# Value casts moved off GpSimd, weight loads released by small gates, and a searched order for the front of an attention and mixture-of-experts kernel

## The chip, the cores and the metric

The kernel runs on one core of one Trainium2 chip. The metric is the device time of one launch in microseconds (us). Engine names are those of the profile: PE is TensorE (PEld its weight loads), DVE is VectorE, ACT is ScalarE, POOL is GpSimd and SP is SyncE, which here only issues transfers. Times are medians over several runs. A ratio is the mean time of one kernel's fast runs over the mean of the other's in the same rounds, so it is not quite the ratio of the medians that stand beside it. A time is about 1.8 us more than the span that the profile shows for the same execution.

## The reference

Shortened here (the logits keep their maximum subtracted, the constants of the scaling are left out):

```python
def _attn_ref(q, k, v):                       # 8 samples, 8 heads, 576 positions, 64 wide
    phi = lambda x: np.where(x > 0, x, np.exp(x) - 1.0) + 1.0
    q_p, k_p = phi(q), phi(k)
    kv = np.einsum('bhsd,bhse->bhde', k_p, v)
    z = np.sum(k_p, axis=2)
    num = np.einsum('bhsd,bhde->bhse', q_p, kv)
    den = np.einsum('bhsd,bhd->bhs', q_p, z)[..., None] + 1e-06
    return num / den
def _moe_ref(x, w_gate, w1, w2):              # x 4608 x 512, 8 experts, 1024 hidden
    P = np.exp(x @ w_gate - max)              # then 8 rounds of row and column scaling
    ...
    for e in range(8):
        out += P[:, e:e+1] * (np.maximum(x @ w1[e], 0) @ w2[e])
```

## The kernel before

A planner in the kernel's own Python takes a list of tasks, each with an engine, a modelled duration, its dependencies and a rank (`prio`). It simulates the engines and emits every task on its engine in the order of that simulation. Only the order comes from it. On the chip each engine runs its list in that order, and waits come from the tiles.

```python
pick = ...   # of the tasks that can start first on this engine: the lowest (prio, id)
t["fn"](e)   # emit it
```

The front is attention in 16 half batches (sample b, four heads g). TensorE does it interleaved with the two layers of expert 0. The loads of half batches 2 and 3 are issued by GpSimd, the others by SyncE, and the value cast is on GpSimd:

```python
(nc.gpsimd if n in (2, 3) else nc.sync).dma_start(out=<kin, qin, vin>, in_=...)
...
tvv.append(fadd(("pool", 1.3), f_v, deps=[ta, tin["v"]], use=[gvv, gin["v"]], prio=pr))   # fp32 -> fp16
...
w_t = {0: load_w1(0, prio=-290.0, parts=2, deps=[vcast[0]])}       # w1 of expert 0
w_t[0] += load_w2(0, prio=-96.5, parts=2, deps=[in_prev[0]])       # w2, behind half batch 3's loads
w_t[1] = load_w1(1, prio=0.0, after=110.0) + load_w2(1, prio=0.0, after=115.0)
```

The softmax here doesn't subtract the row's maximum and nothing guards it: scores larger than these inputs give would overflow.

## Time and profile before

| | before |
|---|---|
| time, median of 3 | 981.74 us (981.48 to 982.49) |
| the profiled execution | 983.97 us, span 982.2 |
| TensorE busy | 98% of the span |
| VectorE, ScalarE, GpSimd busy | 79%, 57%, 13% |

This document uses, as the prediction does, the **unused TensorE time** of a stretch, because a busy share hides small holes. It is the stretch's length less the sum over its matmuls of their start-to-start time when nothing is waited for (0.2167 us for 128x512, 0.109 for 128x256, and so on). It counts waits, half-speed stretches and warm-up alike. A matmul that crosses a cut is counted in both stretches. So a value can be slightly negative, and sums over many stretches come out too low (27.5 us up to 120 us in the first profile of before, 29.8 if each matmul is counted once). Differences between two kernels move by up to 0.7 us for this reason.

### The profile page before, as it was taken

To read this page: it belongs to the slowest core of one execution; us is meant where nothing else is said; L and a number is where in the kernel's file an instruction comes from. 1 tells how busy PE (TensorE), PEld (TensorE's weight loads), DVE (VectorE), ACT (ScalarE), POOL (GpSimd) and SP (SyncE) were. 2 spreads that over 40 slices of the span, in tenths; PEclk is the share of its full clock that TensorE was granted. 3 is DMA by queue.
4 is the path that set the end of the run, shared out by engine and by line. 5 is a ranking of instruction groups with operands and counts; after the bars stand their busy time and mean duration, and the time that the engine had idled before them with its cause. 6 is when DMAs were issued, how large, how long until landed. Compare 5 with 4: busy or idle time off the path is not lost.

```text
span 982.2 us, 21403 instructions
## 1 busy us (share of the span) xinstructions
PE 962.2 (98%) x8716; PEld 792.7 (81%) x8716; DVE 771.7 (79%) x1561; ACT 563.2 (57%) x1034; POOL 127.9 (13%) x171
## 2 busy tenths in 40 slices
PE   7899999999999999999999999999999999999997
PEld 4455564488888888888888888888888888888885
DVE  6898869967777777777777777777777777777774
ACT  4798754565555555555555555555555555555552
POOL 4111200001111111111111111111111111111110
PEclk9999999999999999999999999999999999999999
DMA  9886953162226312272225322272225322236663
GB/s 318 257 303 239 265 160 140 65 127 77 75 76 142 97 73 76 76 161 76 77 75 137 101 76 75 76 162 76 76 76 137 102 76 76 76 103 168 161 161 98
DMA packets 47029, 121.99 MB, mean 124 GB/s; under 512 B 4177, under 2 KB 18001, under 8 KB 46929
## 3 DMA queue, kind: packets, MB, share of 16 engines
q1 hardware_dynamic: 32128, 99.76, 30.3%
q0 software_dynamic: 14480, 20.33, 11.5%
q8 instruction: 68, 1.11, 0.5%
q10 hardware_dynamic: 320, 0.52, 0.1%
q14 instruction: 33, 0.26, 0.1%
HBM read 119.69 MB, written 17.69 MB: 140 GB/s over the span
## 4 chain that ended last, share of the span: by engine, by line
PE 89%; DVE 1%; ACT 1%; issue 0%
PE ye L809 33%; PE hq L627 23%; PE att L627 11%; PE Zye L627 6%; PE Zye L809 6%; PE ye L706 5%; PE hq L536 4%; PE xt_ps L387 0%; PE kv_ps L306 0%; PE num_ps L371 0%; PE lg_ps L405 0%; DVE tk L281 0%; PE qt_ps L332 0%; ACT tq L272 0%; PE den_ps L347 0%; ACT qpT L221 0%
## 5 line engine op out<-in xcount | busy, mean ns | idle before, releaser
L823 DVE SCALAR_TENSOR_TENSOR acc<-ye,P_sb,acc 128x256 f32<-128x256 f32 x620 | 264.9, 477 | 95.3 <-PE ye L809 77.9
L627 PEld LDWEIGHTS <-W 128*128 128x128 f16 x2016 | 197.1, 98 | 23.7
L809 PEld LDWEIGHTS <-S 128*128 128x128 f16 x1984 | 194.1, 98 | 22.7 <-issue 0.3
L809 PE MATMUL ye<-T,S 128*128 128x256 f16 x1488 | 192.8, 273 | 0.1
L833 POOL TENSOR_TENSOR acc<-acc,st 128x256 f32<-128x256 f32 x124 | 87.5, 725 | 625.6 <-ACT st L830 620.7
L653 ACT ACTIVATE h<-hq 128x512 f16<-128x512 f32 x126 | 76.3, 606 | 160.8 <-PE hq L627 160.8
L627 PEld LDWEIGHTS <-w 128*128 128x128 f16 x1512 | 147.6, 98 | 23.3 <-issue 1.0
L809 PEld LDWEIGHTS <-h 128*128 128x128 f16 x1488 | 145.6, 98 | 16.8
L627 PE MATMUL hq<-xs,W 128*128 128x256 f16 x1008 | 151.2, 273 | 0.0
L627 PE MATMUL att<-xs,W 128*128 128x256 f16 x1008 | 151.2, 272 | 0.0
L627 PE MATMUL hq<-xs,w 128*128 128x256 f16 x1008 | 140.7, 272 | 0.8 <-DVE h L656 0.8
L782 DVE TENSOR_TENSOR S<-h 128x1024 f16<-128x1024 f16 x124 | 85.4, 688 | 57.9 <-ACT h L653 57.9
L656 DVE CUSTOM_DVE_ANT_0 h<-att,s 128x512 f16<-128x512 f32 x126 | 86.7, 688 | 13.1 <-ACT s L643 13.1
L830 ACT ACTIVATE st<-Zye,P_sb 128x256 f32<-128x256 f32 x124 | 52.1, 471 | 78.0 <-PE Zye L809 78.0
L643 ACT COPY s<-hq 128x512 f32<-128x512 f32 x126 | 75.0, 595 | 36.7 <-PE hq L627 36.7
L650 ACT ACTIVATE h<-Zye 128x512 f16<-128x512 f32 x126 | 75.2, 597 | 35.1 <-PE Zye L627 35.1
L656 DVE CUSTOM_DVE_ANT_0 h<-hq,s 128x512 f16<-128x512 f32 x126 | 86.5, 686 | 0.8 <-PE hq L627 0.7
L639 ACT COPY Zye<-hq 128x512 f32<-128x512 f32 x126 | 73.3, 581 | 16.3 <-PE hq L627 16.3
L706 PE MATMUL ye<-w,h 128*128 128x512 f16 x320 | 77.6, 379 | 0.9 <-DVE acc L223 0.9
L627 PE MATMUL Zye<-xs,w 128*128 128x256 f16 x504 | 75.6, 273 | 0.0
L647 ACT COPY s<-att 128x512 f32<-128x512 f32 x126 | 74.5, 591 | 0.0
L536 PE MATMUL hq<-xT,w 128*128 128x512 f16 x288 | 70.6, 379 | 2.4 <-ACT h L540 2.2
(90 smaller groups left out, 963.1 us busy)
## 6 DMA issues: line engine op xcount, KB each, us to landing
xs<-xd SPq DMA_DIRECT2D x63, 896.0 KB, 4.6
w<-in_moe_w_dram POOLq DMA_DIRECT2D x14, 1024.0 KB, 11.7
out_dram<-acc SPq DMA_DIRECT2D x68, 128.0 KB, 2.4
kin<-in_k_dram SPq DMA_DIRECT2D x14, 576.0 KB, 6.0
qin<-in_q_dram SPq DMA_DIRECT2D x14, 576.0 KB, 5.0
vin<-in_v_dram SPq DMA_DIRECT2D x14, 576.0 KB, 6.4
xd<-xst SPq DMA_DIRECT2D x9, 512.0 KB, 2.6
xd<-xT SPq DMA_DIRECT2D x9, 256.0 KB, 7.1
```

Source lines behind the costliest of these rows:

```text
L536: nc.tensor.matmul(ghq["tile"], lhsT=gw1["tile"][:, c, ts(f, P)], rhs=xT[:, c, ds(512 * g, 512)], start=(c == 0), stop=(c == NDT - 1))
L627: nc.tensor.matmul(dst[:, p, :], lhsT=lhs(p, c), rhs=rhs(c), start=(first and p == 0 and c == 0), stop=(c == 1), skip_group_check=True)
L643: nc.scalar.copy(out=gs2["tile"], in_=gX["tile"])
L647: nc.scalar.copy(out=gs5["tile"], in_=gR["tile"])
L650: nc.scalar.activation(out=hd(0, 0), in_=Zt[1], func=AF.Relu)
L653: nc.scalar.activation(out=hd(1, 0), in_=gX["tile"], func=AF.Relu)
L656: nc.vector._custom_dve(TENSOR_ADD_SAT, out=dst, in0=ps, in1=sb, s0=3.0e38, s1=0.0)
L706: nc.tensor.matmul(gy[tt]["tile"], lhsT=gh["tile"][:, f, ds(P * tt, P)], rhs=gw2["tile"][:, f, :], start=(f == 0), stop=(f == NFT - 1))
L782: nc.vector.tensor_tensor(out=Sx[:, i], in0=a0, in1=a1, op=op)
L809: nc.tensor.matmul(bank(g_)[:, s, :], lhsT=lhs(s, kk), rhs=rhs(kk), start=(new and s == 0 and kk == 0), stop=(kk == 3), skip_group_check=True)
L823: nc.vector.scalar_tensor_tensor(out=dst(), in0=bank(g_)[:, s, :], scalar=P_sb[:, gg, e:e + 1], in1=dst(), op0=ALU.mult, op1=ALU.add)
L833: nc.gpsimd.tensor_tensor(out=dst(), in0=dst(), in1=gst["tile"], op=ALU.add)
```

## The change

Its intent is to take the casts off GpSimd, where they hold VectorE up, to let GpSimd issue weights when a four-column copy has seen some value tile arrive, to split the first two layer-1 blocks in halves, to give the exp tiles a third buffer, and to replace the ranks of some 260 tasks by values found in an off-line search over the planner's own model.

```diff
-    p_e = S_.pool(2)
+    p_e = S_.pool(3)                                   # exp tiles, also bufs=3
-        tvv.append(fadd(("pool", 1.3), f_v, ...))
+        tvv.append(fadd(("act", 1.17) if n < 2 else ("dve", 0.75), f_v, ...))
+        if n in (0, 13, 15):
+            def f_gate(_):
+                nc.gpsimd.tensor_copy(out=gate, in_=gin["v"]["tile"][:, 0, 0, 0:4])
+            gates[n] = add(("pool", 0.15), f_gate, deps=[tin["v"]], use=[gin["v"]], prio=pr)
-    w_t = {0: load_w1(0, prio=-290.0, parts=2, deps=[vcast[0]])}
+    w_t = {0: load_w1(0, prio=-290.0, parts=2, deps=[gates[0]])}
+        if g == 0:                                     # layer 1: two halves for the first two blocks
+            jobs = [(f, c, c + 2) for c in (0, 2) for f in range(2)] + jobs[2:]
-    w_t[1] = load_w1(1, prio=0.0, after=110.0) + load_w2(1, prio=0.0, after=115.0)
+    w_t[1] = load_w1(1, prio=0.0, deps=[gates[13]]) + load_w2(1, prio=0.0, deps=[gates[15]])
+    ranks = """
+        45:-90.9997 68:-96.9976 69:-91 70:-97.006 ...      (task:rank[:engine]; cut)
+        ... 1060:8.3482 1061:-97.003 1063:-89.9994
+    """
+    for w in ranks.split():  ...  t["prio"] = float(p)
```

## The prediction

> **What bounds the kernel now.** I read the page first: busy shares, the slices, the chain that ended last.
>
> ```profile
> PE 962.2 (98%) x8716; PEld 792.7 (81%) x8716; DVE 771.7 (79%) x1561; ACT 563.2 (57%) x1034; POOL 127.9 (13%) x171
> PE   7899999999999999999999999999999999999997
> ...
> DMA  9886953162226312272225322272225322236663
> ...
> PE 89%; DVE 1%; ACT 1%; issue 0%
> ```
>
> TensorE is busy for 98%, and its row falls under 9 only in the first two and the last slice. The chain is TensorE for 89%. But a matmul's span overlaps the next one's, so "busy" hides small holes. So I cut the first 140 us into stretches (columns: stretch, length, PE, PEld, DVE, ACT, POOL busy with counts, granted clock, DMA share, GB/s).
>
> ```profile
> 0.00:10.00 10.00, 6.26 (x35) 2.64 (x35) 4.92 (x11) 4.16 (x4) 2.79 (x9) 1.00 0.81 300
> 10.00:20.00 10.00, 8.65 (x91) 5.25 (x92) 8.86 (x20) 5.31 (x10) 8.27 (x11) 0.83 1.14 302
> 20.00:30.00 10.00, 6.55 (x64) 3.40 (x62) 7.17 (x14) 5.88 (x8) 2.74 (x3) 1.00 1.12 305
> 30.00:40.00 10.00, 9.77 (x104) 5.83 (x102) 7.37 (x18) 6.57 (x14) 1.15 (x1) 1.00 1.09 360
> 40.00:50.00 10.00, 8.95 (x107) 5.47 (x106) 9.57 (x17) 9.03 (x16) 1.68 (x1) 1.00 0.52 178
> 60.00:80.00 20.00, 17.59 (x174) 10.27 (x172) 19.45 (x36) 19.31 (x31) 3.96 (x4) 1.00 0.88 300
> 120.00:140.00 20.00, 20.00 (x278) 13.39 (x276) 12.42 (x33) 11.13 (x23) 0.00 (x0) 1.00 0.62 130
> ```
>
> The front (16 half batches of attention, with expert 0's layers between them) has all the holes. DMA is full from 10 to 40 us; DVE and ACT are nearly full from 40 to 80. From 120 us TensorE is never idle until the last unit, and the experts 1 to 7 that follow are unchanged. So the change is worth exactly the TensorE time it saves in the front.
>
> How much is there? I take start-to-start times from the timeline instead of spans: twenty 128x512 matmuls from 140.35 to 144.67 us give 0.216 each. One half batch is 0.62 (18 kv_ps) + 0.51 (9 qt_ps) + 0.27 (10 den_ps) + 0.57 (10 num_ps) + 0.57 (10 xt_ps) = 2.54, times 16 = 40.6 us. Expert 0 is 576 x 0.2167 = 124.8. Logits 4 x 0.9 and column sums 8 x 0.14 add 4.7: 170.1 us of real work. At 208.55 us TensorE has done all of that and 76 matmuls of 0.109 (8.3): 178.4. So about 30 us were not used. With the counts of each line in each stretch the same sum gives the loss by stretch: 9.4 (0 to 10), 6.6 (10 to 20), 4.9 (20 to 30), 4.2 (30 to 80), 1.5 (80 to 120); the remaining 3.5 is spread over stretches without a named wait. The 34 warm matmuls sit in these holes and cost nothing that I can see. By wait (engine and line, released by what: us in total, times, longest) the visible holes are many and small:
>
> ```profile
> PE qt_ps L332 <- DVE tq L281: 2.6, 2, 1.6
> PE kv_ps L306 <- POOL vv L225: 2.2, 1, 2.2
> PE hq L536 <- ACT h L540: 2.2, 3, 1.4
> PE xt_ps L387 <- DVE xn L376: 1.4, 3, 0.8
> ```
>
> **What the Trainium skill says.** "SBUF — State Buffer", section "Who interferes with whom": VectorE shares a port pair with GpSimd, and a VectorE instruction with two SBUF inputs, or in a 2-port mode, waits for a GpSimd instruction that holds it. The trace agrees:
>
> ```profile
> 6.60 1.43 DVE L281 SCALAR_TENSOR_TENSOR tk<-kin,ek 128x576 f16<-128x576 f32 x2
> 12.39 1.15 POOL L225 CAST vv<-vin 128x1152 f16<-128x1152 f32 x1 [0.28 <-DMA vin<-in_v_dram]
> 12.41 2.40 DVE L281 SCALAR_TENSOR_TENSOR tk<-kin,ek 128x576 f16<-128x576 f32 x2
> ```
>
> The same two instructions take 1.43 us alone and 2.40 beside a Pool cast: nearly the cast's own 1.15 more.
>
> "VectorE: DVE Perf Modes", section "The perf-mode tier table (the rule you actually need)": an fp32 copy in SBUF runs at 2 elements a cycle, fp16 tensor_scalar at 4, tensor_tensor at 2. With about 150 fixed cycles at 0.96 GHz (section "Side-by-side: where the cycles go for N=2048 bf16"), 1152 elements are 456 ns at 4x and 757 at 2x; the trace has 0.45 (L275) and 0.76 (L278). So my estimate for the new cast on VectorE, which the trace does not have, is 0.76 us. On ACT it should be the 1.17 of the exp and of the add of the same 1152 elements.
>
> "DMA: Bandwidth & Descriptors", section "Issuing engines are not separate DMA queues": all issuers share the same 16 DMA engines. So a load issued sooner while the DMA row is full moves others back. The 302 to 360 GB/s from 10 to 40 us fit that.
>
> **The change part by part.**
>
> Casts off Pool. Removed: 16 casts, 19.8 us on Pool, which has time. Of the interference, 22 L281 spans on k average 923 ns against a clean 0.76 or so: 3.6 us; on q 16 x (814 - 760) = 0.9; the L275 spans on k 16 x (550 - 450) = 1.6 and on q 0.7. About 6.8 us of VectorE time comes back. Added: 14 x 0.76 = 10.6 us on VectorE and 2 x 1.17 on ACT. So VectorE gets 4 us more work over 120 us, and ACT 2.3. By itself this is no gain in throughput; it removes random 1 us delays and frees Pool's queue, which issues the inputs of half batches 2 and 3 and the first weights.
>
> Gates. A 4-column copy on Pool now releases the weights. For expert 0 the gate follows the arrival of v at 7.9 us instead of the end of the cast at 9.07: weights about 1 us sooner. For expert 1 the loads come some us before the 112 us of now and are first needed near 195: nothing on TensorE.
>
> Split of the first two layer-1 blocks. In the built order, two matmuls on the first two chunks of x now stand before the second half batch's transposes, then 14 follow. It can move 4 x 0.2167 = 0.87 us of work into a hole.
>
> Ranks. The table changes only the order. The built order has the same 17 + 17 warm matmuls, and interleaves attention pieces of 2, 4 or 5 matmuls between expert blocks of 4, finer than before. I walked it by hand with the trace's durations: tq of half batch 0 (now ACT add plus 0.76 instead of 1.43) is ready near 9.95 us against 10.84; kv_ps of half batch 1 starts near 14.5 to 15 against 17.44; its xT lands near 22.5 against 23.6; the first two relus run near 24.2 against 25.64; the second half batch pair's qt_ps near 28.2 against 29.49, with 18 layer-1 matmuls behind it instead of 12. That is 1.3 us sooner plus 6 x 0.217 = 1.3 us more work: 2.6 us gained by 30 us.
>
> From 30 to 120 us 5.7 us of holes remain to be had. A better order should take about half, 2.9, since the searched order was made on modelled durations and every engine runs its list in order. The sum is 2.6 + 2.9 = 5.5 us, so 981.74 - 5.5 = 976.2.
>
> **Rivals.** (a) The new bound is VectorE: from 60 to 80 us it is busy for 19.45 of 20 us already, and the casts add to that. For it: the added 10.6 us. Against: 6.8 come back and 80 to 120 has slack (17.3 of 20). It would make 979 to 983. (b) DMA hides it: the bytes to 40 us are unchanged at a full DMA row, so half batches 2 and 3 arrive when they did (v at 22.95 and 27.25 us). Then only later holes are won: 978 to 979. (c) The search is nearly perfect on the chip too: all 5.7 us of later holes and 5 of the first 30: 971. The first 9 us (arrival at 4.91, exp, VectorE) stay in any case. (d) A weight or x block late for expert 1: against it, 80 us of slack for the loads.
>
> **Range and chances.** The holes total 26.6 us to 120 us, of which at least 15 are startup, so even (c) ends near 971. Two per cent is 19.6 us; beyond what can be won. A loss of 19.6 would need the front to be 70% worse in holes. Predicted 976.2, from 971.5 to 980.5; faster 0.01, same 0.98, slower 0.01.
>
> **What would show it.** L281 spans should be 1.43 per pair everywhere; the new cast 0.76 on VectorE and 1.17 on ACT; first layer-1 matmul near 20.5 us against 22.53, 18 or more of them by 30 us against 13; the sum of PE waits in the front lower by some us; from expert 1 on the same trace, shifted. The prediction is wrong if VectorE, not TensorE, is without holes from 40 to 100 us, if new waits on ACT's queue appear, or if anything after 210 us differs in length.

## More of the kernel before

Experts 1 to 7 read x from nine blocks of 512 rows, g = 0 to 8, in device memory. Each is stored raw and, in a second transfer, with sums made on VectorE in a tile that has two buffers:

```python
def f_raw(_):                                   # SyncE, source lines L555, L556 (L567, L568 after)
    nc.sync.dma_start(out=xd[g][:, 0:512]..., in_=xT[:, 0:2, t0:t0 + 256])
    nc.sync.dma_start(out=xd[g][:, 512:1536]..., in_=xT[:, 2:4, t0:t0 + 512])
ti = add(("sp", 0.2), f_raw, deps=<attention of these rows> + [t_close], prio=0.0)
...                                             # VectorE fills xst, L568 (L580 after)
def f_st(_):                                    # SyncE, L574 (L586 after)
    nc.sync.dma_start(out=xd[g][:, 1536:NXB], in_=gt_["tile"]...)
```

`t_close` is a dependency of the plan only. Nothing on the chip waits for it.

## The result, and the profile after

The changed kernel takes **987.93 us** (986.04 to 988.66, 4 runs) against 981.69 (981.48 to 982.49, 4 runs). The ratio is 1.0059 (95% interval 1.0042 to 1.0076), which is within 2% and therefore "same". But it is a slowdown of some 6 us where a gain of 5.5 was predicted, and above every time that the prediction allowed for (971.5 to 980.5).

The page of the changed kernel, at the places that the prediction shows of before (busy, TensorE in 40 slices, chain by engine):

```profile
PE 964.5 (98%) x8716; PEld 792.5 (80%) x8716; DVE 769.2 (78%) x1559; ACT 569.8 (58%) x1052; POOL 114.8 (12%) x158
...
PE   7999997999999999999999999999999999999997
...
PE 86%; DVE 1%; SPq 1%; ACT 1%; DMA 0%; issue 0%; DVEq 0%; ACTq 0%
```

The third slice, which was 9, is still 9 and the second has risen from 8 to 9. The front is better. A new hole stands in the seventh slice (148 to 173 us), and "SPq", the queue of SyncE, has come into the chain with 1%. Cut into stretches (columns as in the prediction), first before at 140 us, then the changed kernel:

```profile
140.00:160.00 20.00, 20.00 (x117) 9.97 (x115) 17.79 (x48) 9.16 (x17) 0.00 (x0) 1.00 0.56 215
```

```profile
20.00:30.00 10.00, 9.09 (x81) 4.49 (x79) 8.13 (x17) 8.53 (x13) 0.71 (x1) 1.00 1.09 336
...
140.00:160.00 20.00, 13.76 (x60) 6.15 (x59) 10.40 (x29) 6.09 (x11) 0.00 (x0) 0.89 0.64 217
160.00:180.00 20.00, 20.00 (x92) 9.42 (x91) 15.18 (x44) 9.50 (x16) 0.00 (x0) 0.93 0.41 160
```

From 20 to 30 us TensorE is busy for 9.09 us instead of 6.55. From 140 to 160 it was never idle before and now lacks 6.2 us, and its granted clock is 0.89 and then 0.93. The waits of TensorE up to 240 us in the changed kernel (total, times, longest):

```profile
PE cs_ps L446 <- DVE gs L441: 6.2, 1, 6.2
PE kv_ps L309 <- ACT vv L221: 3.1, 2, 2.7
...
PE qt_ps L335 <- DVE tq L281: 0.9, 1, 0.9
...
PE hq L545 <- ACT h L549: 0.7, 2, 0.5
```

Of the small waits the one of hq has shrunk from 2.2 to 0.7. The 0.9 of qt_ps is no gain of the change, though the first profile of before has 2.6: a second profile (e9 below) has 0.9 too. kv_ps now waits 3.1 us for ScalarE's cast, where it waited 2.2 (2.0 in the second profile) for GpSimd's. One wait of 6.2 us is new. The same as unused TensorE time, cumulative, for the kernels that matter below (worked out from the counts of each line in each stretch):

| up to us | before, first profile | before, second profile | after | e1 | e5 | e11 |
|---|---|---|---|---|---|---|
| 10 | 9.4 | 9.7 | 10.0 | 9.6 | 9.8 | 9.7 |
| 30 | 20.9 | 19.9 | 18.1 | 17.8 | 17.7 | 17.9 |
| 40 | 21.2 | 20.3 | 18.6 | 21.0 | 17.9 | 18.0 |
| 120 | 27.5 | 25.7 | 21.9 | 25.1 | 21.7 | 21.3 |
| 140 | 27.4 | 25.5 | 21.5 | 24.8 | 21.3 | 21.0 |
| 180 | 26.7 | 24.5 | 30.0 | 23.9 | 20.7 | 20.0 |
| 240 | 25.7 | 23.9 | 29.3 | 24.7 | 21.7 | 19.2 |
| span | 982.2 | 980.5 | 985.9 | 981.6 | 977.3 | 975.5 |

Against the first profile of before, the changed kernel was 5.9 us ahead at 140 us, as predicted, and 3.6 us behind at 240. The spans differ by 3.7, so nothing more happens later.

### What stands in the hole at 150 us

SyncE's queue before, cut to its turning points (start, duration, issue):

```profile
103.92 0.64 SPq L555 DMA_DIRECT2D xd<-xT  x1
...
140.35 2.16 SPq L574 DMA_DIRECT2D xd<-xst  x2
```

and after:

```profile
136.36 0.37 SPq L567 DMA_DIRECT2D xd<-xT  x1
...
147.58 0.67 SPq L568 DMA_DIRECT2D xd<-xT  x1
148.42 1.01 SPq L586 DMA_DIRECT2D xd<-xst  x2
```

Before, the raw stores of the nine blocks go out from 103.92 us on, as the attention finishes each. Fifteen are gone by 126.2 us and the last three go out by 139.1. After, none goes out before 136.36, then all eighteen follow each other, and the first store of sums comes only at 148.42, 8.1 us later than before. Meanwhile VectorE has filled both buffers of xst and stands at the third:

```profile
151.83 0.42 DVE L580 TENSOR_TENSOR xst<-xT 128x512 f16<-128x512 f16 x1 [8.56 <-DMA xd<-xst]
```

VectorE runs its list in order, so the column sums (gs) that TensorE needs stand behind that, and TensorE waits:

```profile
149.37 1.03 PE L718 MATMUL ye<-w,h 128*128 128x512 f16 x4
156.63 0.56 PE L446 MATMUL cs_ps<-gs,ones_t 128*128 128x8 f32 x2 [6.24 <-DVE gs L441]
157.05 6.35 PE L718 MATMUL ye<-w,h 128*128 128x512 f16 x16
```

After the wait TensorE runs at half speed for a while: 16 matmuls from 157.05 to 163.24 take 0.387 us each on average instead of 0.2167, which is 2.7 us more. With the wait that is 8.9 of the 9.2 us that the table shows lost between 140 and 180 (8.5 in the changed kernel, -0.7 before).

The cause in the source is one entry of the table, `1061:-97.003`. Task 1061 is the raw store of x block 8, the last one. It needs the attention of the last sample. With a rank of -97 the planner puts it ahead of the other eight raw stores, whose rank is 0. In the planner's model this does no harm, because there every one of these tasks waits for `t_close`, the end of all attention. On the chip only block 8 has to wait that long, and SyncE works its list in order.

### The profile page after: what moved, and what is told of

Read it like the earlier page. It is cut to its first block, busy times and chain, and to the rows that moved or that the text cites. A ratio compares the mean times of both kernels' runs of the same rounds, so it can differ in the third digit from the quotient of the medians.

```text
span 985.9 us, 21375 instructions
## 1 busy us (share of the span) xinstructions
PE 964.5 (98%) x8716; PEld 792.5 (80%) x8716; DVE 769.2 (78%) x1559; ACT 569.8 (58%) x1052; POOL 114.8 (12%) x158
## 4 chain that ended last, share of the span: by engine, by line
PE 86%; DVE 1%; SPq 1%; ACT 1%; DMA 0%; issue 0%; DVEq 0%; ACTq 0%
PE ye L821 33%; PE hq L639 23%; PE att L639 11%; PE Zye L639 6%; PE Zye L821 5%; PE ye L718 4%; PE hq L545 3%; SPq L568 1%; SPq L567 0%; DMA xd<-xst 0%; PE num_ps L374 0%; DVE h L668 0%; PE xt_ps L390 0%; DVE xst L580 0%; ACT kvz L221 0%
## 5 line engine op out<-in xcount | busy, mean ns | idle before, releaser
L718 PE MATMUL ye<-w,h 128*128 128x512 f16 x320 | 81.1, 389 | 0.2 <-DMA w<-in_moe_w_dram 0.2
```

Source lines behind the costliest of these rows:

```text
L718: nc.tensor.matmul(gy[tt]["tile"], lhsT=gh["tile"][:, f, ds(P * tt, P)], rhs=gw2["tile"][:, f, :], start=(f == 0), stop=(f == NFT - 1))
```

## The experiments

"Half batch n" is n = 2b + g. Every kernel gave the right result. The kernel before in the same rounds took 981.8 to 982.2 us. A cited TensorE order was compared instruction by instruction in the built programs.

### First call: the two suspects after the first reading

**e1_no_raw_rank**, the changed kernel without the entry.

```diff
-        ... 1060:8.3482 1061:-97.003 1063:-89.9994
+        ... 1060:8.3482 1063:-89.9994
```

> The changed kernel without one of the 260 entries, the one that puts the store of the last x block (block 8) at the head of SyncE's queue. Theory A (queue order): the last block's store waits for the end of attention at 136 us, and all other x stores behind it with it, so VectorE stalls 8.6 us on the x-combination buffer, TensorE 6.2 us on the first column sums, and its clock falls. Then this run is 975 to 977.5 us, VectorE has no wait on the x-combination store over 1 us, the granted clock is 1.00 from 140 to 180 us, and the front keeps its 5.9 us. Rival B (the searched order of the tasks after attention is itself late on VectorE): it stays at 984 to 988. Rival C (the x stores are slow because they share the DMA engines): it stays above 982, with the stall a few us long.

TensorE's order is the changed kernel's but for a few instructions (54 of 17,410 lines compared differ, none of them in the front). Measured: 982.96 us (980.64 to 983.40, 5 runs), ratio 1.0004 (0.9992 to 1.0017). The stall at 150 us is gone and 5.0 us come back, but the expected gain over before does not appear. Its profile shows a second loss, which the profiled run of the changed kernel happened not to have in full (TensorE, the second half of w2):

```profile
35.17 0.39 PE L374 MATMUL num_ps<-kvz,qpT 128*128 128x128 f16 x4
37.68 1.82 PE L718 MATMUL ye<-w,h 128*128 128x512 f16 x4 [2.12 <-DMA w<-in_moe_w_dram]
39.52 1.85 PE L718 MATMUL ye<-w,h 128*128 128x512 f16 x4
```

TensorE waits 2.12 us for the weights and then does four matmuls in 1.82 us instead of 1.02, at half clock. In the table this is the jump from 17.8 to 21.0. A further 1.3 us is lost at 200 to 220 us, where without the entry the plan puts block 8's sums on VectorE ahead of what expert 1 needs.

**e2_before_raw8_first**, the kernel before with only that order changed. TensorE's order is identical to before.

```diff
-        ti = add(("sp", 0.2), f_raw, deps=deps + [t_close], prio=0.0)
+        ti = add(("sp", 0.2), f_raw, deps=deps + [t_close], prio=-97.0 if g == NG - 1 else 0.0)
```

> The kernel before with one priority changed: the store of x block 8 is put first in SyncE's queue. Theory A: this alone makes the stall: VectorE waits 7 to 10 us on the x-combination store near 145 us, TensorE loses as much plus some 2.5 us of low clock, and the time is 988 to 992 us. Rival B: no change beyond 1 us, 981 to 982.5.

Measured: 987.01 us (986.87 to 987.45, 4 runs), ratio 1.0053 (1.0039 to 1.0067). One store moved ahead in SyncE's queue costs 5.2 us by itself. The size is a little under what was expected because the column sums are waited for 3.2 us here, not 6.2.

**e3_no_ranks**, the changed kernel without the whole table.

```diff
-    ranks = """ ... """   (and the loop that applies it)
```

> The changed kernel without the whole rank table: casts on VectorE and ACT, gates, split layer-1 blocks and a third exp buffer stay. SyncE's order is that of before, so theory A has no stall after attention. If the front's 5.9 us come from the ranks, this is 979 to 982; if they come from the casts, the gates and the split, it is 976 to 978. VectorE beside no cast on Pool has L281 at 1.43 a pair in either case.

Measured: 983.05 us (980.89 to 984.68, 5 runs), ratio 1.0012 (0.9998 to 1.0026). Both expected ranges are missed. Without the table the kernel is as slow as before, and it too waits for w2, 1.96 us in its profile. So this second loss does not come from the table.

**e4_st_on_act**, the changed kernel with its whole table, and the stores of the sums issued by ScalarE. TensorE's order is identical to the changed kernel's.

```diff
-            nc.sync.dma_start(out=xd[g][:, 1536:NXB], in_=...)
+            nc.scalar.dma_start(out=xd[g][:, 1536:NXB], in_=...)
```

> The changed kernel with the whole table; only the stores of the x combinations are issued from ACT's queue instead of SyncE's. Theory A: the stores no longer stand behind the eighteen raw stores, so VectorE's wait shrinks from 8.6 us to under 2 us, and the time is 976 to 979 us although the raw stores are as late as before. Rival C (the DMA engines are the limit): the stores land late all the same, the wait stays over 5 us and the time at 984 or more.

Measured: 980.04 us (978.17 to 981.67, 4 runs), ratio 0.9981 (0.9967 to 0.9994). The stores of sums no longer stand behind the raw stores and 7.9 us come back. The time lies between what the theory (976 to 979) and its rival (984 or more) allowed, nearer to the theory. The late raw store itself does no harm. The wait for w2 is still there, without the half clock this time:

```profile
37.60 1.02 PE L718 MATMUL ye<-w,h 128*128 128x512 f16 x4 [1.91 <-DMA w<-in_moe_w_dram]
```

A wait of 2.12 us was followed by half speed in e1, one of 1.91 (and 1.96 in e3) was not. These kernels spread over 2.8 to 3.8 us from run to run where the kernel before spread over 0.8 in the same rounds.

### Second call: why w2 comes late

In the changed kernels ScalarE and VectorE free the input buffers sooner, so SyncE issues half batch 4's three loads at 22.7 to 28.2 us instead of 26.7 to 30.0 (1.8 MB, while the DMA row is full). The issue of w2 begins at 17.5 to 18.3 us (in e3 at 16.0, its second half at 17.7), and the later landing of its two halves took 15.6 us from issue before and 19.1 in e1.

**e5_hb4_behind_w2**, e1 with these three loads behind w2 on GpSimd's queue. TensorE's order is identical to e1's.

```diff
-                (nc.gpsimd if n in (2, 3) else nc.sync).dma_start(
+                (nc.gpsimd if n in (2, 3, 4) else nc.sync).dma_start(
```

> The changed kernel without the rank of x block 8's raw store, and with the three loads of half batch 4 issued from Pool's queue behind w2 of expert 0 instead of SyncE's, so that they cannot share the DMA engines with it. TensorE's order is the same as in e1_no_raw_rank. Theory (the loads of half batches 4 and 5, issued some 4 us sooner, push the landing of w2 back): the wait of the second w2 group near 37.7 us (2.12 us in e1, then a half-speed clock) goes, the stretch 30 to 40 us loses under 1.5 us instead of 3.26, and the time is 978 to 980.5. Rival (w2 is late because of something that Pool does, not for the shared engines): the wait stays at 1.5 us or more and the time stays at 981 to 984. Second rival: half batch 4 itself comes so late that TensorE waits for it between 40 and 60 us, and the time stays at 981 to 984 with the w2 wait gone.

Measured: 979.17 us (978.98 to 980.24, 6 runs), ratio 0.9976 (0.9963 to 0.9988). The wait is gone, the same matmuls follow each other without one:

```profile
35.72 1.02 PE L718 MATMUL ye<-w,h 128*128 128x512 f16 x4
...
36.70 1.02 PE L718 MATMUL ye<-w,h 128*128 128x512 f16 x4
```

The stretch 30 to 40 us loses 0.2 us instead of 3.3, the time falls by 3.8 us and the spread shrinks to 1.3 us. The loads themselves are issued hardly later than in e1 (at 23.28, 28.13 and 28.84 us instead of 22.69, 27.32 and 27.80). What changed is their queue. From 26 to 30 us (packets, MB, share of the DMA engines), first e1, then e5:

```profile
q0 software_dynamic: 485, 0.51, 72.4%
q1 hardware_dynamic: 272, 0.59, 42.8%
```

```profile
q0 software_dynamic: 816, 0.84, 123.7%
```

q0 carries what GpSimd issues, w2 among it, and q1 what SyncE issues. In e1 the two share the engines. In e5 nothing is on q1 at that time, q0 moves 0.84 MB instead of 0.51, and w2 lands at most 13.5 us after its issue instead of 19.1. Half batch 4 is not waited for. The rival that looked to GpSimd falls, since GpSimd issued w2 later here (18.15) than in e1 (17.84). What is left is 1.1 us at 197 us:

```profile
197.39 1.03 PE L639 MATMUL hq<-xs,w 128*128 128x256 f16 x8 [0.78 <-DVE h L668]
```

**e6_no_ranks_hb4_behind_w2**, the same edit on e3. TensorE's order is identical to e3's.

> The same move of half batch 4's loads, in the changed kernel without the table at all. Theory: time falls from the 983 of e3_no_ranks by the same 1.5 to 3 us as e5 falls from e1, to 980 to 981.5. If the table is worth something beyond its one bad entry, e5 is faster than this one by 0.5 us or more; if it is worth nothing, the two are within 0.5 us. Rival: no change, 982 to 984.

Measured: 979.36 us (979.16 to 980.07, 5 runs), ratio 0.9976 (0.9963 to 0.9988). It falls by 3.7 us, as e5 fell from e1. With the entry merely deleted the table is worth nothing: 1.4 us better up to 180 us, and 1.7 us worse from 180 to 220.

**e7_hb4_cast0_pool**, e5 with the first cast back on GpSimd.

```diff
-("act", 1.17) if n < 2 else
+("pool", 1.3) if n == 0 else ("act", 1.17) if n < 2 else
```

> As e5, and the first cast (half batch 0) is back on Pool, where it lay in the kernel before; the gate stays. Theory (ScalarE does three things in series before the first product, so kv of half batch 0 starts at 10.0 instead of 9.1 us): kv starts at 9.1 to 9.4, the loss of the first 10 us falls from about 9.6 to 9.1 to 9.4, and the time is 0.4 to 0.8 us under e5. Rival: Pool's cast holds the gate and w1 up behind it, layer 1 starts later and the time is e5's or up to 1 us more.

Measured: 979.77 us (979.62 to 980.34, 5 runs), ratio 0.9979 (0.9966 to 0.9993). It gained nothing. kv_ps starts at 9.64 us instead of 9.82 in e5 and the loss of the first 10 us falls by 0.2 us, but 20 to 30 us loses 1.0 more. The theory of a costly ScalarE at the start falls.

**e8_w2_before_hb3**, e1 with w2 ahead of half batch 3's loads.

```diff
-            w_t[0] += load_w2(0, prio=-96.5, parts=2, deps=[in_prev[0]])
+            w_t[0] += load_w2(0, prio=-97.5, parts=2, deps=[<half batch 2's v load>])
+            S_.dep(<half batch 3's k load>, w_last[0])
```

> As e1, with w2 of expert 0 issued ahead of the three loads of half batch 3 on Pool's queue, instead of behind them; TensorE's planned order changes here, because the planner sees w2 sooner. Theory (w2 late for the queue and the shared engines): no wait on w2 near 37 us, time 978 to 981. Rival: half batch 3's inputs, about 2 us later, hold up the attention and the saving is lost between 25 and 35 us: 981 to 984.

Measured: 1010.94 us (1009.00 to 1012.22, 4 runs), ratio 1.0295 (1.0280 to 1.0309). There is no wait on w2, but everything else is worse: by 240 us it has lost 22 us more than e5, in many waits from 40 us on. The planner saw w2 sooner and rearranged TensorE's order, while the table's ranks still belonged to the old one. Its clock record also has 17 us at half speed between 47 and 265 us. Whether the stale ranks or the late half batch 3 cost more is not separated. So this run does not decide the question that it was made for.

### Third call: the baseline, a control and both mends together

**e9_before_again** is the kernel before, unchanged, for a second profile.

> The kernel before, unchanged, for a second profile of it. Theory: the profiled execution on which the prediction was built took 983.97 us, 2.2 us over the median of the timed ones, so its 27.4 us of unused TensorE time up to 140 us are some 2 us too many; a profile of a usual execution (span 979.8 to 980.6) shows 25 to 26 us, and most of the difference in one or two stretches before 120 us. Rival: the profile costs about 2 us in every run of this kernel, and the second profile shows a span of 982 and the same 27 us again.

Measured: 982.17 us (981.93 to 982.33, 4 runs), with a profiled run of 982.27 and span 980.5. Its unused TensorE time is 25.5 us up to 140 us. The first profile had 27.4. Its run, at 983.97 us, was above every one of the timed runs beside it.

**e10_before_hb4_behind_w2** is the control, the edit of e5 alone on the kernel before. TensorE's order is unchanged.

> Control for e5 and e6: the kernel before with only the loads of half batch 4 moved to Pool's queue behind w2. In the kernel before these loads were issued late anyway (26.7 us and on) and w2 was never waited for. Theory: no gain, 981.5 to 983 (a loss of up to 1 us, since Pool's casts now stand in front of these loads). Rival: the move by itself is worth the 2.5 us that e5 and e6 show against before, and the change nothing: 979 to 980.

Measured: 984.05 us (983.55 to 984.67, 5 runs), ratio 1.0018 (1.0004 to 1.0031). By itself the edit costs 2 us, 1 us more than was allowed for, so it is not what makes e5 and e6 faster than before.

**e11_st_on_act_hb4** has both mends, the edits of e4 and e5, with the whole table. TensorE's order is identical to e4's.

> The changed kernel with its whole table, both faults mended: the combination stores issued from ScalarE's queue (as in e4, so x block 8's raw store holds nothing up) and half batch 4's loads behind w2. TensorE's order is that of e4. Theory: against e4 the 1.9 us wait on w2 goes; against e5 the 1.1 us that TensorE waits at 197 us (VectorE makes x block 8's combinations there) does not come up. 976.5 to 978.5, spread under 1.5 us. Rival: e4's table order has no gain left over e5, 979 to 980.

Measured: **977.38 us** (977.28 to 978.78, 5 runs), ratio 0.9952 (0.9940 to 0.9964). It beats both kernels: 4.7 us under before and 10.6 under the changed kernel. Neither loss is in its profile (last column of the table), nor the 1.1 us of e5.

**e12_casts_on_pool** is e6 with every cast back on GpSimd.

> As e6 (no table, half batch 4's loads behind w2), with all the value casts on Pool as in the kernel before; gates, split layer 1 and the third exp buffer stay. Theory (the cast off Pool is the part that gains): VectorE's stt rows return to the 920 ns of before, the time goes back up by 1.5 to 3 us, to 981 to 982.5. Rival (the gain comes from the gates and the split layer 1): 979 to 980, as e6.

Measured: 987.88 us (985.31 to 988.81, 6 runs), ratio 1.0051 (1.0038 to 1.0065). L281 on k is back at 881 ns, as expected. But the time is far worse than expected, and it does not tell what was asked. With the casts on GpSimd the order of TensorE changes too, and half batch 4's loads, now on the same queue, stand behind casts (its v load at 30.48 us against 26.99 in e6). The clock was at half speed from 50.6 to 57.4 us.

### Fourth and fifth call: what each part is worth

These edits change what the planner sees, so it also makes a new order. Running the planners of the kernels without building them shows how much: of 1,658 TensorE tasks 266 stand in another place in e13 than in e10, 110 in e16 than in e14, and 80 in e17 than in the kernel before. What a part is worth below is therefore its worth together with the order that the planner makes for it.

**e13_before_casts_off_pool** is e10 with the casts moved and no other edit.

```diff
-        tvv.append(fadd(("pool", 1.3), f_v, ...
+        tvv.append(fadd(("act", 1.17) if n < 2 else ("dve", 0.75), f_v, ...
```

> The kernel before with only the value casts moved (ScalarE for half batches 0 and 1, VectorE after), and half batch 4's loads behind w2 so that w2 cannot come late; no gates, no split, no third exp buffer, no table. To be set against e10 (984.05, the same with the casts on Pool). The prediction's step (by itself no gain in throughput): 983 to 985, as e10. Rival (the casts on Pool, with the VectorE instructions that they hold up, are the main loss of the front): 979 to 981, as e6.

Measured: 987.16 us (986.23 to 988.93, 5 runs), ratio 1.0052 (1.0040 to 1.0065). Both theories fall. Two of GpSimd's issues and the stretch from 50 to 60 us (columns as before):

```profile
1.44 1.66 POOL L207 DMA_DIRECT2D w<-in_moe_w_dram  x2
...
31.13 2.18 POOL L207 DMA_DIRECT2D w<-in_moe_w_dram  x2
```

```profile
50.00:60.00 10.00, 7.74 (x62) 3.57 (x60) 6.25 (x14) 6.99 (x14) 0.00 (x0) 0.83 1.07 364
```

w1 of expert 0 goes out at 1.44 us instead of 9.00, among the first inputs, and the cast of half batch 0's values starts at 9.72 us against 8.03 in e16, which has the gates. The 2 MB of expert 1's weights go out at 31 us instead of 112. Before, GpSimd's casts stood ahead of these issues in its queue and held them back. The plan's `deps=[vcast[0]]` and `after=110` hold nothing back on the chip. With every matmul counted once, e13 is 3.8 us behind e16 at 30 us (21.0 unused against 17.2), 3.2 at 50 and 5.5 at 60. So the larger part lies where only the gate on half batch 0 is missing; no run takes the gates out one by one. From 50 to 60 us DMA is still full, attention starves, and the front loses 3.9 us against 1.5 in e16, some of it to the clock of 0.83. This is what the gates on half batches 13 and 15 are for.

**e14_no_split** is e6 without the split of layer 1. TensorE's order differs from e6's only at the split.

> As e6 (no table, half batch 4 behind w2) without the split of the first two layer-1 blocks; TensorE's order differs from e6 only there. The prediction's step (four matmuls, 0.87 us, moved into a hole): up to 0.9 us slower than e6, 979.5 to 980.3. Rival (nothing: the hole is ended by something else): 979.2 to 979.6.

Measured: 979.73 us (979.37 to 980.75, 5 runs), ratio 0.9975 (0.9962 to 0.9989). It is 0.4 us over e6, with ranges that overlap. The two are of different rounds, and their ratios to the kernel before are the same to 0.0001. So the split is worth 0.4 us at most, and this is not settled.

**e15_no_ranks_both_mended** is e11 without the table.

> As e11 without the table: combination stores from ScalarE's queue, half batch 4 behind w2. TensorE's order is e6's. Theory (the table, once its one bad entry does no harm, is worth what e11 is under this): e6's 979.4, so the table is worth about 2.0 us. Rival (the stores on ScalarE's queue are what makes e11 faster than e5): 977 to 978, and the table is worth nothing.

Measured: 979.43 us (979.09 to 979.84, 5 runs), ratio 0.9971 (0.9959 to 0.9984). The table, once its bad entry does no harm, is worth about 2 us, as expected (979.43 less 977.38; by the ratios to the kernel before in each one's rounds 1.9).

**e16_casts_and_gates_only** is e14 with two exp buffers instead of three.

```diff
-    p_e = S_.pool(3)
+    p_e = S_.pool(2)                                   # and bufs=2
```

> As e14 (casts off Pool, gates, half batch 4 behind w2, no split, no table) with two exp buffers instead of three. Theory (with the gates in place, moving the casts gains by itself, against what the prediction said): 979.5 to 981, at most 1 us over e14. Rival (the third buffer carries the gain): 982 to 984.

Measured: 981.75 us (980.55 to 982.15, 5 runs), ratio 0.9994 (0.9980 to 1.0007). It is 2.0 us over e14 and no better than before, between what the theory and the rival allowed. ScalarE's waits up to 130 us point to the buffer, first in e16 and then in e14:

```profile
ACT ek L266 <- DVE tk L281: 2.4, 2, 1.7
ACT eq L266 <- DVE tq L281: 1.9, 3, 0.9
```

```profile
ACT ek L266 <- DVE tq L281: 0.9, 1, 0.9
```

With two buffers the exp waits until VectorE has used up an earlier exp tile, 5.1 us in all with a third such row of 0.8. With three it waits 0.9. In the second profile of before, casts on GpSimd and two buffers, no such row is among the waits of 0.3 us and more; the first profile has one of 1.9 us.

**e17_gates_and_buffer_only** is the kernel before with the gates and the third exp buffer, casts left on GpSimd.

> The kernel before with the gates and the third exp buffer, casts left on Pool, half batch 4's loads on SyncE as before, no split, no table. Theory (the gain is the casts'): 981.5 to 983, no better than before. Rival (the third exp buffer or the gates carry it): 979 to 980.5.

Measured: 982.20 us (981.92 to 985.12, 5 runs), ratio 1.0006 (0.9993 to 1.0019). Together the two are worth nothing while the casts stay.

So the casts need the gates (e13 against e16: 5.4 us) and the third buffer (e16 against e14: 2.0 us). Even the three together gain only with half batch 4's loads behind w2 (e3 against e6: 3.7 us). Casts and buffer without the gates were not run. Against the kernel before in the same rounds they gain 2.5 us (e14). The table adds about 2, and the split at most 0.4.

## Why the prediction was wrong, point by point

**The step that failed** reads: "From 120 us TensorE is never idle until the last unit ... So the change is worth exactly the TensorE time it saves in the front." With it falls "The table changes only the order", which was argued from TensorE's list. The table also moves work between engines (by the planner, 73 tasks run on the other one of VectorE and ScalarE than without it, e3). And one entry turned round SyncE's list: 9.2 us were lost in the profiled run between 140 and 180 us. Alone on the kernel before it costs 5.2 us (e2), and with the queue untied the changed kernel gains 7.9 (e4). Rival (d) named "a weight or x block late for expert 1" and dismissed it by the slack of the loads. The x blocks were indeed not late for expert 1. What counted was the buffer that their stores free, on which VectorE, and behind it TensorE in expert 0, stood.

**Rival (b), DMA**, was given a size (978 to 979) and the wrong sign. That "the bytes to 40 us are unchanged" is right, but their order is not. Loads that go out sooner, on a second queue, push back the one load that TensorE needs next, and this costs 3.7 to 3.8 us (e3 to e6, e1 to e5). The prediction had the principle: from the Trainium skill, "DMA: Bandwidth & Descriptors", section "Issuing engines are not separate DMA queues", which says that all issuers share the same 16 DMA engines, it concluded that "a load issued sooner while the DMA row is full moves others back". It did not ask which load would be moved.

**The front's gain** was right in kind. The interference of casts with VectorE is gone, as the groups show, before (first row) and after:

```profile
L281 DVE SCALAR_TENSOR_TENSOR tk<-kin,ek 128x576 f16<-128x576 f32 x22 | 19.4, 923 | 0.4
```

```profile
L281 DVE SCALAR_TENSOR_TENSOR tk<-kin,ek 128x576 f16<-128x576 f32 x22 | 15.7, 755 | 0.4
...
L223 DVE CAST vv<-vin 128x1152 f16<-128x1152 f32 x14 | 10.5, 747 | 0.4 <-DMA vin<-in_v_dram 0.4
```

and in the changed kernel's timeline the pair that the prediction shows at 12.41 us with 2.40:

```profile
12.56 1.43 DVE L281 SCALAR_TENSOR_TENSOR tk<-kin,ek 128x576 f16<-128x576 f32 x2
```

The instructions take 755 ns instead of 923, and the new cast 747 ns where 0.76 us was estimated. The first layer-1 matmul came at 20.79 us (20.5 predicted, 22.53 before), with 24 of them by 30 us (18 or more predicted, 13 before, 16 in the second profile of before). ScalarE's two casts took 1.144 us each (1.17).

**The size of the gain.** The sum was 2.6 us by 30 us and 2.9 from there to 120. Between the first profile of before and the changed kernel it was 2.8 and 2.8. That agreement is partly luck. The first profile was of a slow execution. Against the second one, e11 gains 2.0 and 2.4, together 4.4 (counted once 2.1 and 3.0), and its time falls by 4.7. Subtracting a gain read from a 983.97 us run from a median of 981.74 was worth about 1 us of error. And the holes were added up wrongly: the "remaining 3.5" is not "spread over stretches without a named wait". It comes from counting matmuls at the cuts twice. Counted once, the same trace gives 9.4, 6.6, 5.0, 5.9 (30 to 80) and 2.9 (80 to 120), in all 29.8 us. So 8.8 us were to be had from 30 us on, not 5.7, and "about half" was a guess at a sum that was too small.

**Where the gain comes from.** "By itself this is no gain in throughput" holds for the casts: with gates alone they give nothing (e16). But the sum then ascribed all 5.5 us to the order. The table is worth about 2, and 2.0 hang on the third exp buffer, for which the prediction had no term. The 2.6 us by 30 us are not the table's either: counted once, e6 without it has 17.5 us unused there, e5 with it 18.2, and the second profile of before 20.3. Rival (a), VectorE as the new bound, did not come about: from 60 to 80 us VectorE was busy for 17.57 us in the changed kernel, 19.45 before.

**Gates.** That there is "nothing on TensorE" from the gates for expert 1 is right for the loads that they issue (at 98 and 116 us). The prediction saw in the gate for expert 0 only weights about 1 us sooner (issued at 8.45 us against 9.00). It overlooked that, with the casts gone from GpSimd's queue, the gates are all that holds the weights back. e13 shows what happens without them.

**What stays open:** why e8 is so slow, whether the split is worth its 0.4 us, and what made the first profiled run of before 2 us longer. By the table, about half of the difference lies before 30 us. Single runs of before at 983.3 to 984.8 us turned up in the later rounds too.

## What to carry to other kernels

When a scheduler or a table decides the order, read the lists of all engines, and those of the issuing queues first: one issue that has to wait holds up everything behind it, and the plan may not show it if it uses a dependency that the chip does not have. When an engine gets faster, ask which transfers it will now start sooner, on which queue, and which more urgent one they will share the DMA engines with. When work leaves an engine that also issues transfers, ask which of them it was holding back. Before counting small holes in a profile, compare its run's time with the timed runs.

## What the Trainium skill lacked or had wrong

- "DMA: Bandwidth & Descriptors", section "Issuing engines are not separate DMA queues", says that issuing from several engines only saves the time it takes to initiate a DMA, usually small. That section lacks that a waiting issue holds up those behind it on its engine: moving nine stores from SyncE's queue to ScalarE's took 7.9 us off (987.93 to 980.04), with the same transfers and the same order on TensorE.
- Neither that section nor "Queues, rings and completion order" on the same page, which describes the queues, gives the advice to put less urgent loads behind urgent ones on one queue: 982.96 to 979.17 us (e1 to e5), with issue times that moved by 0.6 to 1.0 us.
- "TensorE: Matmul & The Clock Gate", section "Why this matters for your kernels", asks for no idle gaps above about 3 us between bursts. Here one wait of 2.12 us was followed by half speed (four 128x512 matmuls in 1.82 us instead of 1.02), while waits of 1.91 and 1.96 us were not. The clock records of these traces change, up to their last entry, at multiples of 3.41 us (half speed in e1 from 37.76 to 41.17). Counted in such steps, e1's wait (35.56 to 37.68) lies within one, while a step ends at 36.2 and 36.1 us, inside the waits of e3 and e4. That fits, but no run tests it. The long case agrees with the page: after 6.24 us, 16 matmuls took 0.387 us each on average.
- No page that was read says how far one profiled execution may lie from the median: 983.97 us here against 981.48 to 982.49, which moved the sum of small holes by 1.9 us.
